# Scores of the later batches in eight 64 by 32 tiles of TensorE, one query copy there, and a new order of the first chunk, in a fused attention and softplus FFN

## The chip, the cores and the metric

The kernel runs on one core of a Trainium2 chip. The metric is the device time of one execution in microseconds, the median of three runs; a profiled execution beside them gives the trace.

## What is computed

Attention over 8 batches, 8 heads, 576 positions and 64 dimensions, with two kinds of mask, followed by a feed-forward layer with a softplus between two matrix products, all in float32. The stride is 32; x is 4608 x 512, w_in 512 x 2048, w_out 2048 x 512:

```python
scores = scale * np.matmul(q, k.transpose(0, 1, 3, 2))
...
mask_local = (rel >= 0) & (rel < stride)
mask_strided = (rel >= 0) & (pos[None, :] % stride == pos[:, None] % stride)
masks = np.stack([mask_local if h < H // 2 else mask_strided for h in range(H)], axis=0)
scores = np.where(masks[None, :, :, :], scores, -1000000000.0)
scores = scores - np.max(scores, axis=-1, keepdims=True)
attn = np.exp(scores)
attn = attn / (np.sum(attn, axis=-1, keepdims=True) + 1e-09)
...
x = np.ascontiguousarray(attn_out.transpose(0, 2, 1, 3)).reshape(B * S, H * D)
...
h = x @ w_in
g = np.maximum(h, 0.0) + np.log1p(np.exp(-np.abs(h)))
return (g @ w_out).astype(np.float32)
```

## The kernel before

**Attention.** Two heads make a pair, so there are 4 pairs to a batch and 32 in all, numbered n = 0 to 31. The host sorts positions so that both masks become bands: a block of 32 queries sees 64 neighbouring keys. A pair's scores are 9 chunks in two places (partitions 0 to 63 and 64 to 127 of an accumulator), 18 matmuls in all. `SPLIT` parts the chunks into part 0 (chunks 0 to 5) and part 1 (chunks 6 to 8). The four pairs of the first batch write both parts into the banks `py` and get their mask from TensorE (L336). From pair 4 on, part 0 goes into bank `ps` and part 1 into the upper half of bank `po`, and VectorE adds the mask (L412). Then come maxima, exponentials, sums, the division, and 16 transposes on VectorE into `pt` (L466). The weighted sums (L534) of a pair share TensorE's turn with the scores of the next pair: that is a joint step.

**Query copies.** A score matmul (L351) contracts over 128 partitions, 64 of head 0 and 64 of head 1. So that the heads stay apart, the queries are laid out in blocks: `lay_out_q` (L261) copies each head's 64 rows into its own columns of `qT` (two copies of 64x576 to a pair), and the other columns hold zeros, written once by the task `z4`. The stationary operand is then 128x64 (two heads by 32 queries), the output 64 partitions high.

**Feed-forward.** 4608 tokens in 9 chunks of 512. For each chunk 16 steps f: `hidden` (L638, 12 matmuls of 128x128 by 512 in fp32r, splitting x and the weights into a high and a low part), `log_part` on ScalarE (L650, L653, L655), softplus on VectorE (L659), `g_high` and `g_low`, and `output` (L678, 12 matmuls into the four banks `py`).

**What sets the order.** Each engine works through its instructions in the order in which the program issues them. For the first chunk, the first two batches and all weight loads, the order is the list `FIRST`. Its names are tasks: q, k, v load a pair's operands (SyncE's queue), D30 is pair 3's query copy for head 0, S31 pair 3's scores of part 1, X, Y, E, Z, x, r, R, M its softmax, T and C the early transposes, V, H, L the weighted sums and the high and low part of x, J4 the scores of pair 4; wi9 loads a piece of `w_in`, ai9, Bi9, di9, hi9, li9 unpack and split it; F, A, u, G, O are the feed-forward steps. `ON_POOL` and `ON_VECTOR` name the tasks that run on GpSimd or VectorE in place of their usual engine. For the rest, `Plan` places tasks by urgency and cost: every four feed-forward steps one task `S{n}` with the scores of pair n and the weighted sums of pair n - 1. `Q{n}` is the query copy, on ScalarE.

Of the kernel before, what the change touches and what calls it, by code (L numbers as in the profile page):

```python
# [35 lines left out]
q0 k0 v2 mask q1 k1 D00 q2 D11 q3 D01 z4 W S01 D21 wi9 X01 k2 D10 Y01 D30 S00 E01 S10 S11 X00 Z01  # L36
Y00 D20 E00 X10 S21 k3 Y10 Z00 ai9 D31 X11 Bi9 wi0 E10 r0 R0 x11 M0 di9 X21 E11 Z10 S20 S30 Y21 E21
ai0 r1 T02 X20 T01 R1 wi3 C02 S31 v0 Y20 X30 hi9 v1 wi1 T00 M1 C01 E20 li9 Y30 ai3 X31 Z20 T11 C00
Z21 V01 x31 r2 T12 V00 C11 H01 wi2 E30 R2 Bi3 M2 E31 T10 L01 C12 V11 C10 Z30 H00 T22 di3 L00 T21
Bi0 wi4 r3 V10 H11 R3 L11 M3 C22 C21 di0 ai1 H10 T20 C20 V21 T32 L10 hi0 v3 H21 T31 Bi1 wo2 C32 ai2  # L40
wo0 V20 L21 T30 H20 C31 q4 C30 li0 L20 V31 hi3 k4 di1 wi6 V30 H30 ai4 H31 li3 hi1 Fa0 ao0 L30 D40
Bi2 L31 F0 Bo0 Bi4 di2 wi5 di4 li1 A0 ao2 Fa1 D41 wi8 wo1 hi4 J4 Ae0 Al0 Bo2 F1 u0 hi2 Gh0 wo4 li4
ai6 li2 A1 wi11 do0 Ae1 ho0 q5 Gl0 Y40 F4 Bi6 lo0 Al1 Y41 A4 do2 u1 wo6 di6 ai5 X4 wo11 Ae4 Gh1 ho2
ao1 Gl1 s4 Al4 O0 v4 u4 Fa2 E4 Bo1 Fa3 hi6 Gh4 do1 li6 wo3 lo2 r4 F2 ho1 F3 ao4 k5 ai11 Gl4 lo1
wo13 Bi5 O1 di5 R4 Bi11 A2 Ae2 Al2 u2 ai8 wi12 A3 di11 Ae3 Bo4 wo8 Gh2 Al3 M4 hi11 do4 wo5 wi10 Gl2
hi5 ho4 li5 F6 A6 D50 u3 li11 Ae6 ao3 P4 ao8 Al6 wo9 lo4 u6 wo15 Bo3 wi7 Bi8 Gh6 wi13 D51 O2 wi14
Gh3 F5 Gl3 A5 ao6 J5 do3 di8 hi8 O4 Bo6 H41 li8 L41 Ae5 wo10 Bo8 ho3 Al5 Y50 H40 k7 Y51 ai10 u5 F9
do6 X5 Bi10 s5 lo3 q6 k6 ai7 Gh5 E5 F8 Gl5 L40 ho6 di10 r5 lo6 hi10 A8 ao5 Gl6 Bi7 do8 O3 li10 Ae8
di7 Bo5 Al8 ai14 hi7 ho8 A9 lo8 wo12 Ae9 O6 u8 F10 do5 R5 Bi14 Al9 li7 M5 Gh8 u9 ai12 ao10 wo7 v5
ho5 Gl8 Bi12 D61 F7 Gh9 A10 Ae10 wi15 O8 Gl9 Al10 P5 D60 u10 lo5 ao9 wo14 Bo10 di12 A7 di14 Gh10  # L50
Gl10 Ae7 Bo9 hi14 J6 Y61 do10 Al7 hi12 u7 H51 O5 li12 ho10 Y60 X6 Gh7 ai13 L51 s6 li14 F11 E6 do9
lo10 ao7 Bi13 A11 di13 r6 Gl7 v6 Bo7 R6 H50 Ae11 M6 Al11 ai15 ho9 F12 k8 q7 do7 lo9 L50 A12 Ae12
hi13 D71 u11 P6 Al12 O10 F14 u12 Gh11 D70 li13 O9 ao14 Bi15 Gl11 J7 di15 A14 Gh12 hi15 ho7 ao15 lo7
Ae14 Y71 Al14 ao11 Y70 li15 u14 ao12 H61 Gl12 X7 O7 s7 Gh14 Bo11 do11 Bo12 L61 Bo14 E7 ho11 do14
Bo15 F13 q8 H60 A13 Gl14 r7 Ae13 lo11 R7 F15 Al13 ho14 L60 do12 u13 ho12 O11 A15 M7 v7 lo12 Qa0
lo14 O12 P7 Ae15 do15 V70 Gh13 k9 Al15 u15 D80 H70 L70 V71 Gh15 H71 v8 D81 L71 O14 Q1 ao13 Bo13
Gl13 QA1 do13 ho13 Qu1 lo13 ho15 Qh1 Gl15 Ql1 O13 Q0 lo15 q9 QA0 O15 Qu0 Qh0 y1 Ob15 Ql0 y0 y2 y3
# [3 lines left out]
D21 D30 r0 r1 hi9 x31 r3 hi0 hi1 ho0 ho2 hi6 D51 Gh3 ho6 r5 Gh8 ho5 D61 ho10 s6 ho9 hi13 ho7 s7  # L61
Gh14 ho11 Gh13 Gh15 ho13 ho15
""".split()
ON_VECTOR = """
D00 D01 z4 D10 C12 M3 C31 li3 D41 hi4 li2 Gl0 lo0 Gl1 Gh4 li6 lo2 Gl4 lo1 hi11 Gl3 li8 Gl5 lo6 hi10
Gl6 li10 ho8 lo8 Gl10 hi14 lo10 Gl7 hi15 lo7 Gl12 Gl14 lo11 D81 y0
# [50 lines left out]
def attention_softplus_ffn(  # L117
# [71 lines left out]
    qT = const.tile([P, 2 * S], F32, name="qT")  # L189
# [32 lines left out]

    def is_local(n):
        return order[n][1] < NPAIR // 2

    def q_of(n):
        return qT_early[n] if n < NPAIR else qT

    def k_of(n):
        return kT_early[n] if n < NPAIR else kT[n % 2]  # L230

    def pt_of(n, a):

        if n in (1, 3):
# [84 lines left out]
    def scores(n, part):  # L319
# [25 lines left out]
        if masked and n > 0:  # L345
            add(True)
# [677 lines left out]
```

## Time and profile before

| | |
|---|---|
| median of 3 runs | 888.06 us (887.53 to 888.86) |
| the profiled execution | 887.86 us, of which span 886.1 us |
| TensorE's granted clock, mean | 0.998 |
| L678 output, busy | 358.5 + 224.1 us |
| L638 hidden, busy | 355.1 + 224.1 us |
| scores from pair 4 on (L351 into ps and po), busy | 25.7 + 14.6 us |
| query copies into qT on ScalarE, busy | 65.6 us in 52 copies |

Times are microseconds of one execution, counted from its first instruction. PE is TensorE, PEld its weight loads, DVE VectorE, ACT ScalarE, POOL GpSimd, SP the engine that issues nearly all DMAs. Busy times of groups overlap and do not add up to the span. A matmul's length in a row is from its start to its modelled end and is longer than the time for which it holds TensorE; what a stretch costs is read from the starts, or from the chain of waits, which follows the work that ended last back to its releasers.

### The profile page before, as it was taken

What the parts mean: (1) busy time and instruction counts of PE and PEld (TensorE: products, weight loads), DVE (VectorE), ACT (ScalarE), POOL (GpSimd) and SP (SyncE); (2) the same over time, 40 slices, a digit from 0 to 9 for tenths busy, and PEclk for the clock granted to TensorE, in tenths of its full rate; (3) what the DMA queues carried; (4) which work ended last, traced back from release to release, by engine and by line L of the source; (5) the groups of instructions that cost most, each with busy time, mean ns of one, the idle gap of its engine ahead of it and who ended that gap; (6) DMA issues with size and microseconds to landing.
All of it is one profiled execution on the core that took longest, in us unless ns stands there. A gap on an engine that the chain in (4) does not pass through costs nothing.

```text
span 886.1 us, 14289 instructions
## 1 busy us (share of the span) xinstructions
PE 874.9 (99%) x5618; PEld 722.5 (82%) x5618; DVE 583.5 (66%) x1289; ACT 432.9 (49%) x762; POOL 71.1 (8%) x92
## 2 busy tenths in 40 slices
PE   7999999999999999999999999999999999999998
PEld 6788888888888888888888888888888888888886
DVE  7899967888766677777766676667777333333332
ACT  6887954544545444544544545444543333333332
POOL 6346550000000000000000000000000000000000
PEclk9999999999999999999999999999999999999999
DMA  9892202211211121111211121112100010001001
GB/s 331 290 371 102 70 31 75 75 46 44 92 45 44 31 76 44 44 45 45 78 45 44 44 92 45 29 31 78 58 18 18 1 48 1 0 1 48 1 0 48
DMA packets 50082, 58.26 MB, mean 66 GB/s; under 512 B 3168, under 2 KB 35296, under 8 KB 50016
## 3 DMA queue, kind: packets, MB, share of 16 engines
q1 hardware_dynamic: 49728, 57.03, 19.8%
q8 instruction: 44, 0.72, 0.3%
q10 hardware_dynamic: 288, 0.33, 0.1%
q14 instruction: 22, 0.18, 0.1%
HBM read 47.91 MB, written 9.44 MB: 65 GB/s over the span
## 4 chain that ended last, share of the span: by engine, by line
PE 97%; DMA 1%; issue 0%; ACT 0%; DVE 0%; SPq 0%; ACTq 0%; DVEq 0%
PE py L678 45%; PE ph L638 44%; PE ps L351 3%; PE pv L534 2%; PE po L534 1%; PE po L351 1%; DMA ri<-in_moe_w_in_dram 1%; PE pt L504 1%; DMA raw_q<-in_qk_dram 0%; PE py L351 0%; ACT a_i L598 0%; DVE a_i L609 0%; PE py L336 0%; DVE qT L261 0%; PE pt L486 0%
## 5 line engine op out<-in xcount | busy, mean ns | idle before, releaser
L678 PE MATMUL py<-w_o,gh 128*128 128x512 f32 x1152 | 358.5, 392 | 0.0
L638 PE MATMUL ph<-x_h,w_i 128*128 128x512 f32 x1152 | 355.1, 389 | 0.0
L650 ACT ACTIVATE u<-ph 128x512 f32<-128x512 f32 x144 | 86.0, 597 | 400.3 <-PE ph L638 397.0
L638 PEld LDWEIGHTS ph<-x_h,w_i 128*128 128x128 f32 x1152 | 215.9, 188 | 45.4 <-issue 0.4
L678 PEld LDWEIGHTS py<-w_o,gh 128*128 128x128 f32 x1152 | 214.0, 188 | 46.6 <-DVE w_o L624 0.2
L638 PE MATMUL ph<-x_l,w_i 128*128 128x512 f32 x576 | 224.1, 389 | 0.0
L678 PE MATMUL py<-w_o,gl 128*128 128x512 f32 x576 | 224.1, 389 | 0.0
L659 DVE SCALAR_TENSOR_TENSOR u<-ph,u 128x512 f32<-128x512 f32 x144 | 99.2, 689 | 176.6 <-ACT u L655 175.0
L466 DVE STREAM_TRANSPOSE pt<-prob 32x192 f32<-32x192 f32 x448 | 137.2, 314 | 6.4
L678 PEld LDWEIGHTS py<-w_o,gl 128*128 128x128 f32 x576 | 108.1, 188 | 22.8
L638 PEld LDWEIGHTS ph<-x_l,w_i 128*128 128x128 f32 x576 | 108.1, 188 | 22.6
L671 DVE TENSOR_TENSOR gl<-u,gh 128x512 fp32r<-128x512 f32 x138 | 95.4, 692 | 11.8 <-DVE gh L261 0.9
L653 ACT ACTIVATE u<-u 128x512 f32<-128x512 f32 x144 | 91.2, 633 | 4.3
L655 ACT ACTIVATE u<-u 128x512 f32<-128x512 f32 x144 | 91.1, 632 | 4.4
L261 ACT COPY qT<-prob 64x576 f32<-64x576 f32 x52 | 65.6, 1261 | 1.0 <-DMA prob<-in_qk_dram 0.7
L261 DVE CAST gh<-u 128x512 fp32r<-128x512 f32 x129 | 54.9, 425 | 10.3
L412 DVE TENSOR_TENSOR prob<-ps,mask_b 128x384 f32<-128x384 f32 x28 | 15.6, 556 | 49.3 <-PE ps L351 49.3
L351 PEld LDWEIGHTS ps<-kT,qT 128*64 128x64 f32 x672 | 21.9, 137 | 10.2 <-issue 8.8
L351 PE MATMUL ps<-kT,qT 128*64 128x64 f32 x672 | 25.7, 226 | 0.3 <-DVE qT L261 0.3
L412 DVE TENSOR_TENSOR prob<-po,mask_b 128x192 f32<-128x192 f32 x28 | 10.0, 356 | 19.6 <-ACT x_h L572 19.6
L570 DVE TENSOR_TENSOR x_l<-pv,x_h 128x288 fp32r<-128x288 f32 (+2 forms) x44 | 17.4, 407 | 5.7 <-ACT x_h L572 5.5
L427 ACT ACTIVATE prob<-prob 128x576 f32<-128x576 f32 x24 | 16.5, 688 | 9.1 <-DVE prob L421 9.1
(102 smaller groups left out, 507.0 us busy)
## 6 DMA issues: line engine op xcount, KB each, us to landing
v_in<-in_v_dram SPq DMA_DIRECT2D x28, 320.0 KB, 3.6
out_dram<-o SPq DMA_DIRECT2D x35, 256.0 KB, 2.1
ri<-in_moe_w_in_dram SPq DMA_DIRECT2D x16, 512.0 KB, 7.8
ro<-in_moe_w_out_dram SPq DMA_DIRECT2D x16, 512.0 KB, 8.2
prob<-in_qk_dram SPq DMA_DIRECT2D x28, 288.0 KB, 2.7
kT<-in_qk_dram SPq DMA_DIRECT2D x28, 288.0 KB, 3.0
v_in<-in_v_dram SPq DMA_DIRECT2D x28, 48.0 KB, 2.7
room<-in_v_dram SPq DMA_DIRECT2D x4, 320.0 KB, 5.9
```

Of the source, the lines that this page charges most:

```text
L261: (engine.copy if engine is nc.scalar else engine.tensor_copy)(dst, src)
L351: nc.tensor.matmul(ps[rows[place], 64 * (x - lo) : 64 * (x - lo) + 64], lhsT=blocks_of(n)[:, c // 32].rearrange("p h l -> p (h l)"), rhs=k ...
L412: nc.vector.tensor_tensor(pv, sv, m, op=ALU.add)
L466: nc.vector.transpose(pt[32 * (i + c) : 32 * (i + c) + 32, h, a : a + hi - lo, 32 * i : 32 * i + 32,], src[:, lo:hi, 32 * c : 32 * c + 32],)
L534: nc.tensor.matmul(po[64 * h : 64 * h + 64, TILE * x : TILE * x + TILE], lhsT=vs[n][:, a, h, :], rhs=pt_of(n, a)[:, h, a % 2], start=True, ...
L638: nc.tensor.matmul(ph, lhsT=w32["i", f][:, half, cc * P : (cc + 1) * P], rhs=x_of(x, cc)[:, t0 : t0 + n], start=(i == 0), stop=(i == 3 * N ...
L650: nc.scalar.activation(us[c, f], phs[c, f], AF.Abs)
L653: nc.scalar.activation(u, u, AF.Exp, scale=-1.0)
L655: nc.scalar.activation(u, u, AF.Ln, bias=1.0)
L659: nc.vector.scalar_tensor_tensor(u, in0=phs.pop((c, f)), scalar=0.0, in1=u, op0=ALU.max, op1=ALU.add)
L671: engine.tensor_tensor(g, us.pop((c, f)), ghs[c, f].bitcast(F32), op=ALU.subtract)
L678: nc.tensor.matmul(py[t], lhsT=g[:, sl], rhs=w32["o", f][:, half], start=(f == 0 and n == 0), stop=(f == NFC - 1 and n == 2),)
```

## The change

Three parts.

1. From pair 4 on, `head_scores` takes the place of `scores`. It issues one matmul for each head: 64 rows (that head's dimensions), 32 columns (32 queries), 64 keys streamed; 36 matmuls to a pair. The output of chunk, place and head goes to the 32 partitions from 64 * place + 32 * `place_of(part, h)`. In part 0 head 0 comes first, in part 1 head 1, so that the four tiles of part 0 and the four of part 1 are eight different tiles of the 128x128 array. Chunks 0 to 2 are issued alone (four tiles), then 3 with 6, 4 with 7, 5 with 8. `prob_transposes` reads the rows accordingly. The first batch keeps its 128x64 scores.
2. As the heads no longer stand side by side in one operand, `qT` holds the queries once: `lay_out_q` is one copy of 128x576, the zeros (`z4`) go, and the tasks D40 and D41 become D4 (the same for 5 to 8).
3. `FIRST`, `ON_POOL` and `ON_VECTOR` are new.

```diff
 FIRST = """
-q0 k0 v2 mask q1 k1 D00 q2 D11 q3 D01 z4 W S01 D21 wi9 X01 k2 D10 Y01 D30 S00 E01 S10 S11 X00 Z01
...
+mask q0 k0 q1 W D00 k1 D10 q2 q3 D01 S01 X01 D11 D20 Y01 S00 S11 X00 S10 Y00 E01 Z01 k2 D31 D21 S20
...
-    qT = const.tile([P, 2 * S], F32, name="qT")
+    qT = const.tile([P, S], F32, name="qT")
...
     def lay_out_q(n, heads=(0, 1), engine=nc.scalar):
 
+        if n >= NPAIR:
+            to = qT.rearrange("p (m l) -> p m l", l=32)
+            copy_on(engine, to, raws[n].rearrange("p (l m) -> p m l", l=32))
+            return
...
+    def place_of(part, h):
+
+        return 1 - h if part == 1 else h
+
+    def head_scores(n):
+
+        taken.append(n)
+        pss[n, 0] = ps_s.tile([P, 512], F32, tag="ps", name=f"ps_{n}")
+        shared[n] = ps_o.tile([P, 512], F32, tag="po", name=f"po_{n}")
+        pss[n, 1] = shared[n][:, S // 2 :]
+        for x in range(6):
+            for chunk in (x, x + 3) if x > 2 else (x,):
+                part = chunk // 6
+                for place in range(2):
+                    a, i = block_at(chunk, place)
+                    c = TILE * a + 32 * i
+                    for h in range(2):
+                        to = 64 * place + 32 * place_of(part, h)
+                        head = slice(64 * h, 64 * h + 64)
+                        at = 64 * (chunk - SPLIT[part][0])
+                        nc.tensor.matmul(
+                            pss[n, part][to : to + 32, at : at + 64],
+                            lhsT=qT[head, c : c + 32],
+                            rhs=k_of(n)[head, c : c + 64],
+                            start=True,
+                            stop=True,
+                        )
...
-                for lo, hi in ((0, 6), (6, 9)):
+                for part, (lo, hi) in enumerate(SPLIT):
+                    row = 64 * place + 32 * place_of(part, h)
+                    src = p[row : row + 32]
...
     def joint_scores(n):
 
-        scores(n, 0)
-        scores(n, 1)
+        head_scores(n)
...
-    task("z4", zeros, NPAIR, of("z4", nc.gpsimd))
...
         def work(i=i, n=n):
-            scores(n, 0)
-            scores(n, 1)
+            head_scores(n)
```

On TensorE, the first joint step of the program (pair 5's scores, then pair 4's weighted sums); the rows give line, operation, output, operands, output size and how many follow each other. Before:

```order
L638 MATMUL ph_5_932<-x_h_592,w_i_856 128x512 x2
L638 MATMUL ph_5_932<-x_l_612,w_i_856 128x512
L351 MATMUL ps_0_951<-kT_101,qT 64x64 x12
L351 MATMUL po_964<-kT_101,qT 64x64 x6
L534 MATMUL po_964<-pt,v_in 64x96 x6
L534 MATMUL pv_977<-pt,v_in 64x96 x6
L678 MATMUL py_104<-w_o_858,gh_4_785 128x512 x2
```

After:

```order
L699 MATMUL py_107<-w_o_774,gl_2_925 128x512
L373 MATMUL ps_978<-kT_101,qT 32x64 x16
L373 MATMUL po_979<-kT_101,qT 32x64 x4
L373 MATMUL ps_978<-kT_101,qT 32x64 x4
L373 MATMUL po_979<-kT_101,qT 32x64 x4
L373 MATMUL ps_978<-kT_101,qT 32x64 x4
L373 MATMUL po_979<-kT_101,qT 32x64 x4
L555 MATMUL po_979<-pt,v_in 64x96 x6
L555 MATMUL pv_1022<-pt,v_in 64x96 x6
L659 MATMUL ph_9_1046<-x_h_363,w_i_888 128x512 x2
```

The 12 + 6 matmuls of 64 partitions have become 24 + 12 of 32 partitions, the last three rounds alternating between the two banks; the weighted sums stand behind them as before.

On SP, which issues the loads, the first rows of the program (raw_q0 to raw_q3 are the queries of pairs 0 to 3; early_l0, l2, l1, l3 the keys of pairs 0, 1, 2, 3; room_2 the values of pair 2; ri_9 a piece of w_in). Before:

```order
L258 DMA raw_q0_149<-in_qk_dram 128x576
L279 DMA early_l0_91<-in_qk_dram 128x576
L290 DMA room_2_111<-in_v_dram 96x128
L297 DMA room_2_111<-in_v_dram 128x5x128
L258 DMA raw_q1_155<-in_qk_dram 128x576
L279 DMA early_l2_93<-in_qk_dram 128x576
L258 DMA raw_q2_159<-in_qk_dram 128x576
L258 DMA raw_q3_162<-in_qk_dram 128x576
L578 DMA ri_9_186<-in_moe_w_in_dram 128x4x128
```

After:

```order
L255 DMA raw_q0_150<-in_qk_dram 128x576
L280 DMA early_l0_91<-in_qk_dram 128x576
L255 DMA raw_q1_153<-in_qk_dram 128x576
L280 DMA early_l2_93<-in_qk_dram 128x576
L255 DMA raw_q2_168<-in_qk_dram 128x576
L255 DMA raw_q3_170<-in_qk_dram 128x576
L280 DMA early_l1_95<-in_qk_dram 128x576
L280 DMA early_l3_97<-in_qk_dram 128x576
L599 DMA ri_1_276<-in_moe_w_in_dram 128x4x128
```

The values of pair 2 and the piece 9 of w_in, which stood among the queries and keys, now stand behind all of them.

On ACT, the rows from the first query copy on (early_h2, h1, h3 are the laid-out queries of pairs 1, 2, 3). Before:

```order
L261 COPY early_h2_92<-raw_q1_155 64x32x18
L377 ACTIVATE early_l0_91<-early_l0_91 128x3x64
L261 COPY early_h1_94<-raw_q2_159 64x18x32
L377 ACTIVATE early_l0_91<-early_l0_91 128x6x64
L598 ACTIVATE a_i_9_249<-ri_9_186 128x512
L261 COPY early_h3_96<-raw_q3_162 64x32x18
```

After:

```order
L258 COPY early_h2_92<-raw_q1_153 64x18x32
L397 ACTIVATE early_l0_91<-early_l0_91 128x3x64
L258 COPY early_h1_94<-raw_q2_168 64x32x18
L397 ACTIVATE early_l0_91<-early_l0_91 128x6x64
L258 COPY early_h3_96<-raw_q3_170 64x18x32
L397 ACTIVATE early_l2_93<-early_l2_93 128x6x64
```

The scaling of weight piece 9 between the copies for pairs 2 and 3 is gone, so pair 3's copy follows pair 0's second exponential directly; the other halves of pairs 2 and 3 are on GpSimd before and after.

81 lines of the change are left out of this document (36 added, 45 removed).

## The prediction

> **What bounds the kernel now.** I read the page first, down to its chain of waits.
>
> ```profile
> span 886.1 us, 14289 instructions
> PE 874.9 (99%) x5618; PEld 722.5 (82%) x5618; DVE 583.5 (66%) x1289; ACT 432.9 (49%) x762; POOL 71.1 (8%) x92
> ...
> PE 97%; DMA 1%; issue 0%; ACT 0%; DVE 0%; SPq 0%; ACTq 0%; DVEq 0%
> ```
>
> TensorE sets the end: 97% of the chain is its own work. Work on DVE, ACT or POOL is worth time only where TensorE waits for it. So next come its three long waits, in square brackets at the end of rows of the timeline, and the busy time by stretch (stretch, length, then busy us of PE, PEld, DVE, ACT, POOL; granted clock, DMA share, GB/s).
>
> ```profile
> 9.36 0.92 PE L351 MATMUL py<-early_l,early_h 128*64 128x64 f32 x24 [1.86 <-ACT early_h L261]
> 12.46 0.91 PE L351 MATMUL py<-early_l,early_h 128*64 128x64 f32 x12 [1.67 <-ACT a_i L598]
> 24.00 0.27 PE L504 MATMUL pt<-room,early_l 128*64 128x64 f32 x1 [1.62 <-issue]
> ...
> 36.00:133.00 97.00, 97.00 (x593) 79.49 (x593) 86.66 (x193) 75.40 (x182) 50.42 (x48) 1.00 0.46 165
> 133.00:690.00 557.00, 557.00 (x3624) 461.03 (x3623) 400.77 (x921) 264.90 (x416) 0.00 (x0) 1.00 0.17 51
> ```
>
> From 36 to 690 us TensorE has no gap at all (97.00 of 97.00, 557.00 of 557.00). The long waits, 1.86, 1.67 and 1.62 us, lie in the first 36 us. So the change can gain in two ways: a shorter score block on TensorE, 28 times over, and a denser head.
>
> **The score block.** The chain of waits around one joint step (last hidden layer, scores, weighted sums, output layer):
>
> ```profile
> 255.11 2.72 PE ph L638 x12
> 257.83 0.85 PE ps L351 x24
> 258.68 0.35 PE po L351 x12
> 259.02 0.50 PE po L534 x12
> 259.52 0.49 PE pv L534 x12
> 260.02 2.94 PE py L678 x12
> ...
> L351 PE MATMUL ps<-kT,qT x672: 222/222/270, 34.5 to 669.4; 128*64 128x64 f32 x168
> L351 PE MATMUL po<-kT,qT x336: 222/222/222, 35.3 to 669.7; 128*64 128x64 f32 x168
> ```
>
> The kernel issues 18 score matmuls to a pair, the trace counts 36 (672 + 336 over 28 pairs): a float32 matmul is two passes. The steady po part runs 12 passes in 0.35 us. Two tiles of 64 columns are in use, so 6 passes follow each other on each and **a pass holds its tile 58 ns**. All 36 are 18 x 0.058 = 1.05 us; the block takes 0.85 + 0.35 = 1.20, so 0.15 is the change from the 128x128 shape to the 128x64 shape. Going back costs 2.94 - 2.72 = 0.22.
>
> That tiles run beside each other, each at its own pace, stands in the head's timeline (start, length, then the operation):
>
> ```profile
> 15.86 0.24 PE L486 MATMUL pt<-room 128*64 128x128 bf16 x2
> 15.91 0.65 PE L504 MATMUL pt<-room,early_l 128*64 128x64 f32 x16
> ...
> 18.56 0.25 PE L534 MATMUL pv<-pt,room 128*64 128x96 f32 x1
> 18.62 0.22 PE L504 MATMUL pt<-room,early_l 128*64 128x64 f32 x1
> 18.65 0.36 PE L534 MATMUL pv<-pt,room 128*64 128x96 f32 x4
> ```
>
> Two 128-column matmuls take 0.05 us together, as long as one pass of 58 ns. And at 18.56 a weighted sum (L534) begins on one tile while the other still has a transpose (L504) to start at 18.62.
>
> After the change there are 36 matmuls to a pair, 72 passes, each over half the rows and half the columns. A pass still streams 64 columns, so I keep 58 ns. The six chunks of part 0 use four tiles: 6 matmuls, 12 passes on each, 12 x 0.058 = 0.70 us. Part 1's three chunks use the other four tiles and fit beside the last three rounds (6 passes, 0.35). New is a second change of shape, from 64x32 to the weighted sums' 128x64. No row shows that pair of shapes; the nearest are 0.15 and 0.22, and I take 0.15, since it leads into the same shape as the 0.15 row. **New block: 0.15 + 0.70 + 0.15 = 1.00, a gain of 0.20** in the 26 joint steps (pairs 5 to 7, 9 to 31). Pairs 4 and 8 have no weighted sums behind the scores and gain 1.05 - 0.70 = 0.35. Sum: 26 x 0.20 + 2 x 0.35 = **5.9 us**.
>
> The bounds: with the second change of shape free, 26 x 0.35 + 0.7 = 9.8; at 0.22, 26 x 0.13 + 0.7 = 4.1. What no row shows is tiles that differ in their rows, or more than two at once; if only two ever run, the passes take 36 x 0.058 = 2.10 and the block is slower (a rival below).
>
> **The query copies.**
>
> ```profile
> L261 ACT COPY qT<-prob x52: 1242/1258/1280, 31.9 to 648.4; 64x576 f32<-64x576 f32 x52
> L219 DVE MEMSET qT<- x2: 538/538/538, 5.8 to 6.5; 64x576 f32 x2
> ...
> L412 DVE TENSOR_TENSOR prob<-ps,mask_b 128x384 f32<-128x384 f32 x28 | 15.6, 556 | 49.3 <-PE ps L351 49.3
> ```
>
> One copy over 128 partitions replaces two over 64, from the second batch on: about 28 x 1.26 = 35 us less copying, nearly all on ACT. It is worth nothing in the loop, because TensorE never waits there. The DVE transposes and mask adds keep their number and sizes. Both parts of the scores now end together, so the first mask add cannot begin ahead of the second part; DVE has room for that (400.77 busy of 557.00). If that cover were gone, one mask add, 0.56 us by its row, would stand in each step. The two memsets go, which belongs to the head.
>
> **The head.** Here the order counts. The rows of ACT and POOL at the two early waits, the loads by size, and the stretches:
>
> ```profile
> 8.14 1.16 ACT L261 COPY early_h<-raw_q 64x576 f32<-64x576 f32 x1 [5.76 <-DMA raw_q<-in_qk_dram]
> ...
> 9.60 1.25 ACT L261 COPY early_h<-raw_q 64x576 f32<-64x576 f32 x1
> ...
> 11.67 0.66 ACT L598 ACTIVATE a_i<-ri 128x512 f32<-128x512 f32 x1 [0.39 <-DMA ri<-in_moe_w_in_dram]
> 12.35 1.23 ACT L261 COPY early_h<-raw_q 64x576 f32<-64x576 f32 x1
> ...
> 9.64 2.52 POOL L261 COPY early_h<-raw_q 64x576 f32<-64x576 f32 x2 [3.11 <-DMA raw_q<-in_qk_dram]
> ...
> ri<-in_moe_w_in_dram SPq DMA_DIRECT2D x16, 512.0 KB, 7.8
> ...
> room<-in_v_dram SPq DMA_DIRECT2D x4, 320.0 KB, 5.9
> ...
> room<-in_v_dram SPq DMA_DIRECT2D x4, 48.0 KB, 6.1
> ...
> 8.00:12.00 4.00, 1.43 (x40) 1.24 (x40) 3.66 (x9) 3.44 (x5) 2.30 (x2) 0.98 1.05 387
> 12.00:14.00 2.00, 1.54 (x25) 1.52 (x27) 1.76 (x7) 1.95 (x3) 1.37 (x3) 0.50 1.08 383
> 14.00:16.00 2.00, 2.00 (x51) 1.95 (x49) 1.81 (x5) 1.95 (x9) 1.38 (x4) 0.68 1.14 355
> 16.00:20.00 4.00, 3.97 (x127) 3.89 (x124) 3.23 (x10) 3.36 (x8) 3.11 (x5) 1.00 1.10 371
> 20.00:24.00 4.00, 2.38 (x75) 2.24 (x70) 4.00 (x10) 2.47 (x11) 1.18 (x2) 1.00 1.09 393
> ```
>
> The DMA engines are full here (share 1.05 and more). The first wait (to 9.36 us) is for pair 1's query, copied at 8.14; ahead of it stand the 48 + 320 KB of a value load, 377 kB at 387 GB/s = 1.0 us. The new order sends values and weights behind all queries and keys: 1.0 earlier. The second wait (from 10.79, 1.67 before 12.46) is for pair 3's second half, copied on ACT at 12.35, behind a weight scaling that itself stood behind its 512 KB load. In the new order ACT has no weight work there, and pair 3's halves follow pair 2's on ACT and POOL. The first copies then run from 9.60 - 1.0 = 8.6 to 9.85, the second to 11.1. TensorE, itself 1.0 earlier, ends pair 1 at 9.8, works some 1.2 us on pair 2 (36 passes on two tiles, 1.05, and mask adds), and meets pair 3 at 11.1: about 1.6 of the 1.67 is gone. Together 2.6. DVE is nearly full after that (10.80 busy of 12 us from 12 to 24), and though it sheds two memsets (1.08), I take 0.3 off: **2.3 us**. The third wait (1.62, where nothing in the profile released TensorE) I leave as it is. The weight loads that now come later on SP cost nothing as long as the first weights are ready by the first hidden layer; one load of w_in stands before the values and one among them, so I count none.
>
> Clock: after the two gaps it reads 0.50 and 0.68, about 2 x 0.50 + 2 x 0.32 = 1.6 us of TensorE time lost. I count no gain there, because DVE would bind instead. The Trainium skill, page "TensorE: Matmul & The Clock Gate", section "What's actually happening", says that the clock drops to half after an idle window of some 3.4 us and knows nothing between half and full. The 0.50 agrees; by that rule the denser head never throttles, and the sum would come out up to 1.6 lower.
>
> Ends for the head: 2.3 + 1.6 (clock) + 1.6 (third wait gone) = 5.5 of gain; a second stall like the third wait leaves 0.7; and an order that gains nothing, 0.
>
> **Sum.** The profiled execution took 887.86 us (span 886.1, 1.8 around it), 0.2 below the median of the runs. 887.86 - 5.9 - 2.3 = **879.7 us**. Its own range is 876 (9.8 and 2.3, or 5.9 and 5.5, about) to 883 (4.1 and 0.7).
>
> **Rivals.**
> - *The head gains nothing* (DVE binds, or a new wait): 887.86 - 5.9 = 882.0. For it: DVE's 4.00 of 4.00 from 20 to 24 us. Against it: both waits named above have their cause moved.
> - *Eight tiles never run at once*, only four: then part 1's passes come on top, 0.15 + 1.05 + 0.15 = 1.35 in place of 1.20, 26 x 0.15 = 3.9 lost, nothing won in the two others. With the head 887.86 + 3.9 - 2.3 = 889.5. No row shows more than two tiles at work, which leaves it open.
> - *Tiles of the two row halves take turns on one accumulator bank*: in part 0 the heads sit in different row halves and write into one bank. If they alternate, 12 passes become 24, 1.40 us, and the block 1.70: 26 x 0.50 + 2 x 0.35 = 13.7 lost, 887.86 + 13.7 - 2.3 = 899.3, **slower**. It decides from 0.90 us of passes on (0.15 + 0.90 + 0.15 = 1.20). For it speaks no row; every tile today spans all rows. Against: today's two tiles write different partitions of one bank and do not hinder each other. The Trainium skill, page "TensorEngine Tiling (Array Packing)", section "Restrictions and Gotchas", says that different row tiles cannot use the same PSUM bank at the same time; no run here shows it yet.
> - *Passes start no faster than now*, one every 29 ns: 72 take 2.10, the change does not do what it says, 26 x 1.20 + 2 x 1.05 = 33.3 lost, 918.9. The starts at 18.62 and 18.65 on tiles of their own speak against a common beat. The first page named, section "Wait — 56ns, not 53.3ns?", gives a floor of about 25 ns between starts; by it, an estimate, 72 passes take 1.8 us and the kernel ends near 910.
>
> **Chances.** Forecast 0.65, head gains nothing 0.17, four at once 0.07, bank turns 0.06, no faster starts 0.05. The first two are faster by over 0.2% (1.8 us, about what a measurement here can tell from no change): 0.82. Four at once lies within: 0.06, the other 0.01 of it with the slower ones, 0.12. The first two hold 0.82, so the range is theirs: 875.5 to 886.0, its upper end past 882.0 by 4, for a head that loses a stall or two.
>
> **What would show it.** Right: the score rows of a joint step sum to 1.0 us in the chain of waits, po's rows lie inside those of ps, the waits on L351's early copies fall to some tenths, and the first hidden matmul starts some 2.3 us earlier than now. Wrong: a block of 1.35 or 1.70 (turns), a longer first row of the weighted sums (the second change of shape), or a new TensorE gap between 12 and 60 us with DVE or a weight load as its releaser.

## The result and the profile after

The changed kernel takes 884.25 us (median, 882.83 to 884.51) against 888.44 (887.53 to 888.86) for the kernel before on the same chip: a ratio of 0.9949, 95% interval 0.9937 to 0.9961. The forecast was 879.7 with a range of 875.5 to 886.0. So it became faster, by about half of what was forecast. The profiled execution took 884.07 us, 3.79 less than that of before; the forecast was 8.2 less.

The page of the changed kernel: the span, the engines' busy time with their instructions, the engines' shares of the chain of waits, the instruction queues, and the query copies.

```profile
span 882.3 us, 16274 instructions
PE 872.7 (99%) x6626; PEld 717.4 (81%) x6626; DVE 585.7 (66%) x1283; ACT 403.0 (46%) x742; POOL 65.8 (7%) x88
...
q8 instruction: 52, 0.85, 0.4%
...
PE 93%; DMA 2%; DVE 2%; ACT 1%; issue 1%; POOL 0%; SPq 0%; ACTq 0%; POOLq 0%
...
L258 ACT COPY qT<-prob 128x576 f32<-128x576 f32 x26 | 33.2, 1278 | 1.5 <-DMA prob<-in_qk_dram 1.5
```

TensorE still sets the end. It has 1008 score passes more (28 pairs x 36), and as many weight loads. ACT is 29.9 us less busy. The query copies alone fell by 32.4 us: 52 of 1261 ns (65.6 us) became 26 of 1278 (33.2 us).

The chain of waits around one joint step (start, length, engine, tile, line):

```profile
255.30 0.41 PE ps L373 x20
255.72 0.03 PE po L373
...
256.17 0.12 PE po L373 x8
256.29 0.65 PE po L555 x12
256.94 0.49 PE pv L555 x12
257.43 2.94 PE py L699 x12
...
279.42 0.41 PE ps L373 x20
```

The score rows run from 255.30 to 256.29, 0.99 us in place of 1.20. The first row of the weighted sums grew from 0.50 to 0.65; that is the second change of shape, 0.15. The block is 1.14: a gain of 0.06, where 0.20 was forecast. The way back to 128x128 costs the same as before (2.94). From score row to score row (here 255.30 to 279.42) a joint step takes 24.11 us in place of 24.17, as the median over the loop; this is called the joint period below.

The head: stretches (length, busy us of each engine with its instructions, granted clock, DMA share, GB/s), and TensorE's long waits there, in brackets at the end of the timeline's rows.

```profile
0.00:12.00 12.00, 9.87 (x145) 6.02 (x147) 8.80 (x19) 6.58 (x9) 8.97 (x34) 1.00 0.87 306
12.00:16.00 4.00, 2.68 (x84) 2.44 (x80) 3.92 (x14) 2.94 (x11) 2.11 (x3) 1.00 1.13 355
...
36.00:133.00 97.00, 96.61 (x701) 79.12 (x700) 88.04 (x189) 74.46 (x183) 47.09 (x44) 1.00 0.47 166
133.00:690.00 557.00, 557.00 (x4509) 458.45 (x4509) 403.05 (x921) 234.49 (x391) 0.00 (x0) 1.00 0.17 51
...
7.89 0.57 PE L343 MATMUL py<-early_l,early_h 128*64 128x64 f32 x12 [0.25 <-issue]
9.90 0.92 PE L343 MATMUL py<-early_l,early_h 128*64 128x64 f32 x24 [0.26 <-issue]
...
16.48 0.27 PE L525 MATMUL pt<-room,early_l 128*64 128x64 f32 x2 [1.42 <-issue]
...
22.40 0.22 PE L525 MATMUL pt<-room,early_l 128*64 128x64 f32 x1 [1.36 <-issue]
...
27.54 0.73 PE L659 MATMUL ph<-x_h,w_i 128*128 128x512 f32 x2
```

The waits of 1.86 and 1.67 us on the early copies have become tenths, and the clock stays at 1.00, where it read 0.50 and 0.68 from 12 to 16 us. But where one wait of 1.62 us had no releaser (such waits are called stalls below), there are now two, of 1.42 and 1.36. The first hidden matmul starts at 27.54 us, against 29.19 before: 1.65 earlier, where 2.3 was forecast. Behind the head a gap of 0.4 us is new, at 75 us (96.61 busy of 97.00).

Two things were open. Why do the score passes take 0.84 us (0.99 less the 0.15 for the first change of shape) and not 0.70? And what is the head worth by itself, with its two stalls? The experiments go after one, then the other.

### The profile page after: what moved, and what is told of

Same layout as the page of the kernel before. It is cut to its first block, busy times and chain, and to the rows that moved or that the text cites. A ratio compares the mean times of both kernels' runs of the same rounds, so it can differ in the third digit from the quotient of the medians.

```text
span 882.3 us, 16274 instructions
## 1 busy us (share of the span) xinstructions
PE 872.7 (99%) x6626; PEld 717.4 (81%) x6626; DVE 585.7 (66%) x1283; ACT 403.0 (46%) x742; POOL 65.8 (7%) x88
## 4 chain that ended last, share of the span: by engine, by line
PE 93%; DMA 2%; DVE 2%; ACT 1%; issue 1%; POOL 0%; SPq 0%; ACTq 0%; POOLq 0%
PE py L699 43%; PE ph L659 42%; PE pv L555 2%; DMA ro<-in_moe_w_out_dram 2%; PE ps L373 2%; PE po L555 2%; PE po L373 1%; PE pt L525 1%; DVE pt L487 0%; DMA raw_q<-in_qk_dram 0%; ACT prob L453 0%; DVE early_h L258 0%; DVE u L680 0%; DVE a_o L630 0%; ACT early_h L258 0%
## 5 line engine op out<-in xcount | busy, mean ns | idle before, releaser
L487 DVE STREAM_TRANSPOSE pt<-prob 32x192 f32<-32x192 f32 x448 | 140.2, 317 | 6.7
L692 DVE TENSOR_TENSOR gl<-u,gh 128x512 fp32r<-128x512 f32 x135 | 93.3, 691 | 10.6
L258 ACT COPY qT<-prob 128x576 f32<-128x576 f32 x26 | 33.2, 1278 | 1.5 <-DMA prob<-in_qk_dram 1.5
L373 PEld LDWEIGHTS ps<-kT,qT 64*32 64x32 f32 x1344 | 23.3, 106 | 9.9 <-issue 9.2
L373 PE MATMUL ps<-kT,qT 64*32 64x64 f32 x1344 | 27.8, 220 | 0.0
L373 PE MATMUL po<-kT,qT 64*32 64x64 f32 x672 | 22.0, 227 | 0.0
```

Of the source, the lines that this page charges most:

```text
L258: (engine.copy if engine is nc.scalar else engine.tensor_copy)(dst, src)
L373: nc.tensor.matmul(pss[n, part][to : to + 32, at : at + 64], lhsT=qT[head, c : c + 32], rhs=k_of(n)[head, c : c + 64], start=True, stop=True,)
L487: nc.vector.transpose(pt[32 * (i + c) : 32 * (i + c) + 32, h, a : a + hi - lo, 32 * i : 32 * i + 32,], src[:, lo:hi, 32 * c : 32 * c + 32],)
L692: engine.tensor_tensor(g, us.pop((c, f)), ghs[c, f].bitcast(F32), op=ALU.subtract)
```

## Experiments on the score passes

**Rounds of six.** The twelve matmuls of part 1 are spread over all six rounds, two to a round.

```diff
         for x in range(6):
-            for chunk in (x, x + 3) if x > 2 else (x,):
+            for chunk in (x, 6 + x // 2):
                 part = chunk // 6
-                for place in range(2):
+                for place in (range(2), (x % 2,))[part]:
```

> Six rounds of six matmuls in place of three of four and three of eight: in each round the four of part 0, then two of part 1 (both heads of one place, the places taking turns). A tile of part 0 comes again after 12 passes and not after 16. In the changed kernel the 72 passes of a joint score block took about 0.85 us and the block 1.14. Window theory (TensorE looks only about 16 passes ahead; with eight tiles in a round the second pass of a tile blocks all that stand behind it): the passes run at 56 ns on every tile of part 0, 12 x 0.056 + 0.03 = 0.70 us, block 0.99, joint period 24.11 - 0.15 = 23.96, kernel 28 x 0.15 = 4.2 us less than the changed kernel, near 880.0. Rival A, a floor of about 12 ns a pass as soon as more than four tiles are used: 72 x 0.012 = 0.86, no gain, 884.2. Rival B, two tiles over one another in the same columns hinder each other: the same 12 matmuls of part 1 still share columns with part 0, so the loss stays, 0.86, 884.2.

Measured: 881.42 us, ratio 0.9916 (0.9901 to 0.993). One score block in its chain of waits:

```profile
277.25 0.19 PE ps L373 x4
...
278.10 0.06 PE po L373 x2
278.15 0.65 PE po L555 x12
```

The score rows take 0.90 in place of 0.99, and the joint period is 24.03. The gain is 0.09, between the 0.15 of the window theory and the zero of rivals A and B. None of the three holds as it was put.

**Rounds of four only**, and **four with two tiles in the same columns.** In the first, part 1 comes after all of part 0:

```diff
-        for x in range(6):
-            for chunk in (x, x + 3) if x > 2 else (x,):
+        for x in range(9):
+            for chunk in (x,):
```

> The six rounds of part 0 first, then the three of part 1, never more than four tiles at a time: 9 rounds x 2 x 0.056 = 1.01 us of passes, plus 0.03, so 0.18 more than the changed kernel's 0.85: block 1.32, joint period 24.29, kernel 28 x 0.18 = 5.0 us more, near 889.3. All theories say this; if it takes less, passes on a tile are quicker than 56 ns, if the same as the changed kernel, the rounds of eight gave nothing at all.

In the second, each of the first six rounds has two matmuls of part 0 and two of part 1, one above the other in the same columns:

```diff
-        for x in range(6):
-            for chunk in (x, x + 3) if x > 2 else (x,):
+        for x in range(9):
+            round_ = [(x - 3, place, h) for place in range(2) for h in range(2)]
+            if x < 6:
+                column = x // 3
+                round_ = [(x % 3 + 6 * o, p, column ^ o) for p in range(2) for o in range(2)]
+            for chunk, place, h in round_:
...
```

> Nine rounds of four as in the run beside it, but in the first six of them two tiles stand over one another in the same columns (one matmul of part 0 and one of part 1, from the two halves of the rows, into two banks); the computation is the same. Window theory and rival A (floor per pass): only four tiles at a time, so the same 1.01 + 0.03 us of passes as the run beside it, kernel within 0.5 us of that one, near 889.3. Rival B (tiles in the same columns hinder each other): in the changed kernel three rounds of eight with four such pairs each lost 0.17 us over the 0.67 hoped for, 0.014 a pair and more if pairs take turns; here 12 pairs at turns cost up to 12 x 0.056 = 0.67 more, at least 0.17, kernel 4.8 to 19 us above the run beside it.

Measured: 884.41 us (ratio 0.9952, 0.9937 to 0.9967) and 884.51 (0.9951, 0.9934 to 0.9967), joint period 24.16 in both. Rival B falls: tiles in the same columns cost nothing. But both runs are 5 us below what all theories said, and about level with the changed kernel; as their joint period is that of the kernel before (24.17), what they gain lies outside the joint steps. The chain of the first shows how:

```profile
255.65 0.64 PE ps L373 x36
256.29 0.03 PE po L373
...
256.46 0.23 PE po L373 x13
256.69 0.65 PE po L555 x12
```

The passes took 1.04 - 0.15 = 0.89 us and not 1.04. The first pass of part 1 is the 49th in the program, yet it starts after only 36 passes of part 0: it overtakes 12. (How far TensorE starts later passes past waiting ones is called its look-ahead here.) So part 1 slides over the last rounds of part 0, though no round has more than four matmuls. The timeline of the changed kernel shows the same number:

```profile
303.46 0.48 PE L373 MATMUL ps<-kT,qT 64*32 64x64 f32 x20
303.73 0.24 PE L373 MATMUL po<-kT,qT 64*32 64x64 f32 x1
```

There the first pass of part 1 is the 33rd, and it starts after 20. In both orders the first pass of part 1 went past 12 waiting passes and no more. The same two rows show the rate of the rounds of four: 20 passes in five groups of four, the first 21 starts within 0.27 us. That is the forecast's 56 to 58 ns per pass on each of four tiles.

**Part 1 first, and part 1 brought forward.** Two more orders: in the first, shown against the rounds of six, part 1's matmuls stand ahead in each round; in the second, against the changed kernel, the rounds have 7, 7, 6, 6, 6 and 4 matmuls:

```diff
-            for chunk in (x, 6 + x // 2):
+            for chunk in (6 + x // 2, x):
```

> Rounds of six as in the earlier run of six, but the two matmuls of part 1 ahead of the four of part 0 in each round. There the tiles of part 0 started a pass every 14.7 ns (56 / 4 = 14.0 at best), and after the last of them came two passes of part 1, 0.057 us. Window theory: the tiles of part 0 set the end, the tail goes and the start is 14 ns later: passes 0.72 in place of 0.756 us, joint period 24.03 - 0.04 = 23.99, kernel 1 us below the run of six. Rival (a rate of 10.5 ns a pass whatever the order, 72 x 10.5 = 756): no change, 24.03.

```diff
-        for x in range(6):
-            for chunk in (x, x + 3) if x > 2 else (x,):
+        late = [(6 + y, p, h) for y in range(3) for p in range(2) for h in range(2)]
+        for x, many in enumerate((3, 3, 2, 2, 2, 0)):
+            round_ = [(x, place, h) for place in range(2) for h in range(2)] + late[:many]
+            late = late[many:]
+            for chunk, place, h in round_:
...
```

> Rounds of 7, 7, 6, 6, 6 and 4 matmuls: the twelve of part 1 brought forward, none in the last round. Window theory: a tile of part 0 comes again after at most 14 passes, still inside 16, so these tiles go on at 14 to 14.7 ns a pass to the end and nothing follows them: passes 0.69 to 0.70 us in place of 0.756, joint period 23.97, kernel 1.5 us below the run of six. Rival (10.5 ns a pass whatever the order): 0.756, 24.03, no change.

Measured: 880.96 us (ratio 0.9912, 0.9896 to 0.9929) and 880.72 (0.9912, 0.9897 to 0.9927), joint period 24.03 in both. The window theory's gains of 0.04 and 0.06 a step did not come: three orders give the same 24.03. So something besides the tiles and the look-ahead seems to hold the passes to a rate; the next run tests that.

**Twice the passes for the same columns.** Each matmul of the rounds of six is cut into two of 32 keys.

```diff
-        for x in range(6):
+        for x, side in ((x, side) for x in range(6) for side in range(2)):
...
-                at = 64 * (chunk - SPLIT[part][0])
+                at = 64 * (chunk - SPLIT[part][0]) + 32 * side
+                k0 = c + 32 * side
                 nc.tensor.matmul(
-                    pss[n, part][to : to + 32, at : at + 64],
+                    pss[n, part][to : to + 32, at : at + 32],
                     lhsT=qT[head, c : c + 32],
-                    rhs=k_of(n)[head, c : c + 64],
+                    rhs=k_of(n)[head, k0 : k0 + 32],
```

> The rounds of six once more, but each matmul cut into two of 32 keys: in each round first the six lower halves, then the six upper ones. The same columns stream through the same tiles, in 144 passes in place of 72. In three orders of six and seven the 72 passes took 0.756 us, 10.5 ns each. Rate theory (TensorE takes up passes, or their weight loads, no faster than one in 10.5 ns once its look-ahead is used up): 144 x 10.5 = 1.51 us, joint period 24.03 + 0.76 = 24.79, kernel 28 x 0.76 = 21 us above the run of six, near 902. Rival (the streaming in the tiles sets it, tiles hindering each other while they stream): the columns are the same, 0.76 to 0.85 us, kernel at most 3 us above the run of six, 881 to 884.

Measured: 901.35 us (ratio 1.0135, 1.0088 to 1.0181), joint period 24.51. Its chain of waits gives the whole block, and its timeline a stretch in the middle:

```profile
258.54 0.16 PE ps L374 x4
...
259.89 0.65 PE po L556 x12
```

```profile
308.12 0.23 PE L374 MATMUL ps<-kT,qT 64*32 64x32 f32 x4
308.15 0.21 PE L374 MATMUL po<-kT,qT 64*32 64x32 f32 x1
308.17 0.19 PE L374 MATMUL ps<-kT,qT 64*32 64x32 f32 x1
308.17 0.21 PE L374 MATMUL po<-kT,qT 64*32 64x32 f32 x1
308.18 0.21 PE L374 MATMUL ps<-kT,qT 64*32 64x32 f32 x2
308.20 0.19 PE L374 MATMUL po<-kT,qT 64*32 64x32 f32 x1
308.20 0.21 PE L374 MATMUL ps<-kT,qT 64*32 64x32 f32 x1
308.22 0.19 PE L374 MATMUL po<-kT,qT 64*32 64x32 f32 x1
308.22 0.23 PE L374 MATMUL ps<-kT,qT 64*32 64x32 f32 x4
```

The score rows take 1.35 us, 0.45 more than with half the passes and the same columns. So the number of passes counts, and the rival (streaming) falls. The tiles are not what is full here either: at the start of this block (307.54, 307.57, 307.60 us) part 0's four tiles took a pass each every 0.03 us, and in the stretch shown each takes two in 0.10. The rate is not the 10.5 ns of the expectation, though. The rows repeat after 0.10 us (308.12 to 308.22) with 4 + 1 + 1 + 1 + 2 + 1 + 1 + 1 = 12 passes in between, and that is six matmuls of two passes: **one matmul every 16.7 ns**. All 72 at that rate are 1.20 us, which is 1.35 less the 0.15 for the change of shape. The profiled execution took 898.75 us, 18.3 more than that of the rounds of six (880.46): 28 x 0.48 = 13.4 from the blocks, 1.5 by the first hidden matmul, and 3.1 in stalls without a releaser between 482 and 560 us, of the kind looked at below.

For the blocks of 64 columns 16.7 ns a matmul is not the whole account. Thirty-six matmuls at that rate are 0.60 us, and one part 0 tile's twelve passes 0.67; the runs of six measured 0.75, 0.08 above the larger of the two. The changed kernel would spend 3 x 0.112 = 0.34 us on its rounds of four, where the tiles are the limit, and then 24 x 0.0167 = 0.40 on its rounds of eight, by this estimate 0.74; it measured 0.84. What the remaining 0.08 and 0.10 are, no run shows. What the runs do show is the difference of the orders: part 1's tiles have work from the first round in the runs of six, and that is worth 0.09. What makes the 16.7 ns (taking up instructions, or loading weights) these runs don't tell apart.

## Experiments on the head

**The new scores with the old order.** The changed kernel with the order and engines of the first chunk from before. In the first version the one query copy of a pair stood where the second half had stood (pair 8's on VectorE, as that half had been), in the second version where the first half had stood, all on ScalarE. The second version's list against that of the kernel before (pairs 4 and 5 shown):

```diff
-wo0 V20 L21 T30 H20 C31 q4 C30 li0 L20 V31 hi3 k4 di1 wi6 V30 H30 ai4 H31 li3 hi1 Fa0 ao0 L30 D40
-Bi2 L31 F0 Bo0 Bi4 di2 wi5 di4 li1 A0 ao2 Fa1 D41 wi8 wo1 hi4 J4 Ae0 Al0 Bo2 F1 u0 hi2 Gh0 wo4 li4
+wo0 V20 L21 T30 H20 C31 q4 C30 li0 L20 V31 hi3 k4 di1 wi6 V30 H30 ai4 H31 li3 hi1 Fa0 ao0 L30 D4
+Bi2 L31 F0 Bo0 Bi4 di2 wi5 di4 li1 A0 ao2 Fa1  wi8 wo1 hi4 J4 Ae0 Al0 Bo2 F1 u0 hi2 Gh0 wo4 li4
...
-hi5 ho4 li5 F6 A6 D50 u3 li11 Ae6 ao3 P4 ao8 Al6 wo9 lo4 u6 wo15 Bo3 wi7 Bi8 Gh6 wi13 D51 O2 wi14
+hi5 ho4 li5 F6 A6 D5 u3 li11 Ae6 ao3 P4 ao8 Al6 wo9 lo4 u6 wo15 Bo3 wi7 Bi8 Gh6 wi13  O2 wi14
```

> The new scores with the first chunk's order and engines of the kernel before (the query copies of the later pairs as one, where their second half stood). The two parts of the change add: the scores alone are worth what the joint periods show, 24.17 - 24.11 = 0.06 x 26, and what pairs 4 to 8 gave, about 2 us, kernel near 886.4; first hidden matmul at 29.2 as before, early waits of 1.86, 1.67 and 1.62 us back. Rival: the new order only fits the new scores or the other way round; then the kernel is at 888.4 or above.

> The new scores with the first chunk's order of the kernel before, the single query copies now where the first of the two halves stood, on ScalarE. The earlier run of this kind stood 1.94 us at 60.88 for the query copy of pair 5, which came late. If that wait was the reason why it gained nothing: the wait is gone, the scores are worth 28 x 0.06 = 1.7 us, kernel near 887 (ratio 0.998). Rival (the new scores make the old first chunk slower in another way, its early waits above all, 2.24 us against 1.86): again 888.6 or above, with first hidden matmul at 30 or later.

Measured: 889.54 us (ratio 1.0008, 0.9999 to 1.0018) and 885.21 (0.9952, 0.9938 to 0.9967). The two versions, which differ in the place of five copies, are over 4 us apart. The waits of the first version name 2.3 us of it, and the row behind them has the longest one:

```profile
PE ps L372 <- ACT qT L257: 2.3, 2, 1.9
...
62.81 0.37 PE L372 MATMUL ps<-kT,qT 64*32 64x64 f32 x12 [1.94 <-ACT qT L257]
```

With the copies in time these waits are gone and the old order holds nearly the whole gain. By the spans it is 883.1 us, against 886.1 before and 882.3 for the changed kernel: 3.0 us with the new scores and their single copy, 0.8 more with the order. Not all of the 3.0 is the scores': the first hidden matmul starts at 28.58 us here, 0.6 earlier than before, and at 30.56 in the first version, whose clock was lower in the head (see the rows of both below).

**The old scores with the new order.** The kernel before, with the changed lists; D4 to D8 are again two halves each (shown against the list of the changed kernel).

```diff
-C30 do1 V31 hi1 q4 li1 V30 Fa0 wo2 ai4 Bi4 H30 L30 ho1 ai2 di4 H31 ao0 L31 D4 Bo0 F0 wi3 hi4 Fa1
+C30 z4 do1 V31 hi1 q4 li1 V30 Fa0 wo2 ai4 Bi4 H30 L30 ho1 ai2 di4 H31 ao0 L31 D40 D41 Bo0 F0 wi3 hi4 Fa1
```

> The new order and engines of the first chunk with the scores of the kernel before (each later pair again with two query copies in place of one, at the same place in the order). If the parts add: the score blocks of the changed kernel save 0.06 us each by the joint periods (24.17 to 24.11), 28 x 0.06 = 1.7 us of the 4.2; the first chunk has the other 2.5: kernel near 886.0, first hidden matmul near 27.5. Rival (each order fits only its own scores): the doubled copies on ScalarE hold up scores or outputs of the first chunk, and no more than half of it is left, 887.3 or above.

Measured: 887.21 us, ratio 0.9987 (0.9977 to 0.9996). The first hidden matmul starts at 26.89, but the first chunk has new waits:

```profile
PE ph L638 <- DVE u L659: 1.5, 3, 0.6
PE ps L351 <- ACT qT L261: 0.4, 1, 0.4
```

By the first hidden matmul 2.3 us were won against the kernel before; of these 1.5 are lost again to DVE (the changed kernel loses 0.4 there) and 0.4 to the query copy. So the order is worth 1.2 us with the old scores (0.0013 of 888.65). The rival was nearer: the order fits its own scores better.

**The order's worth once more.** The scores of 7, 7, 6, 6, 6, 4 with the old order, beside the changed kernel itself.

> The rounds of 7, 7, 6, 6, 6 and 4 with the first chunk's order of the kernel before (query copies as in the second run of that kind). What is the new order of the first chunk worth once the scores are the new ones? If the 2.3 us forecast for it hold: 2 us or more above the 880.7 of the same scores with the new order, ratio to the kernel before 0.9912 + 0.0025 = 0.9937. If it is worth what the earlier pair of profiles shows (spans of 883.1 with the old order, 882.3 with the new one): 0.3 to 0.9 us above, ratio 0.9916 to 0.9922. Score blocks as in the run of 7, 7, 6, 6, 6, 4: joint period 24.03.

> The changed kernel itself once more, beside the run above, for the size of the order's worth: ratio to the kernel before 0.9949 as first measured, against 0.9952 for the same scores with the old order. If the new order is worth 2.3 us, its ratio comes out near 0.9926; if 0.3 to 0.9, within 0.994 to 0.995. First hidden matmul between 26.1 and 27.6 us, stalls at the 449th and 705th instruction of 0.5 to 1.6 us each, as in the seven profiles with this order so far.

Measured: 884.41 us (ratio 0.9951, 0.9937 to 0.9965; joint period 24.05) and 883.32 (0.9939, 0.9924 to 0.9954). With the scores of 7, 7, 6, 6, 6, 4 the new order is worth 3.5 us, across two sets of runs (0.9951 - 0.9912 = 0.0039 of 889). With the scores of the change it is 1.2 by the changed kernel's repeat (0.9952 - 0.9939) and 0.3 by its first runs (0.9952 - 0.9949); the intervals are as wide as these differences. Neither answer expected fits both. Part of the spread lies in the old order itself. These rows show the old order with the scores of 7, 7, 6, 6, 6, 4, then in the second version and in the first: a long wait, and the granted clock (third from the end of each second row) from 12 to 16 us.

```profile
11.94 0.91 PE L343 MATMUL py<-early_l,early_h 128*64 128x64 f32 x12 [1.92 <-DMA early_l<-in_qk_dram]
...
12.00:16.00 4.00, 4.00 (x88) 3.89 (x90) 3.50 (x11) 3.19 (x10) 3.05 (x4) 0.66 1.12 369
```

```profile
11.78 0.57 PE L343 MATMUL py<-early_l,early_h 128*64 128x64 f32 x12 [1.70 <-DMA early_l<-in_qk_dram]
...
12.00:16.00 4.00, 3.83 (x124) 3.72 (x122) 3.57 (x12) 3.98 (x13) 2.97 (x4) 1.00 1.12 370
```

```profile
10.26 1.35 PE L342 MATMUL py<-early_l,early_h 128*64 128x64 f32 x24 [2.24 <-ACT early_h L257]
...
12.00:16.00 4.00, 3.01 (x50) 2.69 (x50) 3.73 (x11) 3.40 (x10) 3.08 (x3) 0.50 1.10 369
```

In three of four profiles with the old order (before among them) the clock falls to half, each time for 3.4 us or twice that. It is not the length of one wait alone. In the kernel before the clock stayed at 1.00 through the wait of 1.86 us and fell at 11.9 us, within the next one, of 1.67. With the scores of 7, 7, 6, 6, 6, 4 it fell at 11.4, within the wait of 1.92 that followed two of 0.9, and again at 25.0, behind a stall of 1.89. In the first version it fell at 10.5, right behind the wait of 2.24, and stayed at 1.00 through the wait of 1.94 that ended at 62.81. In the second version waits of 1.20, 0.98 and 1.70 left it at 1.00. With the new order it read 1.00 from 12 to 16 us in every profile. That fits the new order winning more where the old one loses its clock, and little where it does not.

**The two stalls.** Dummies are matmuls whose result nobody reads; the program issues ten ahead of the first scores. Here there are sixty-four more, each narrower, so that the stretch is as long but 128 instructions are ahead of everything.

```diff
-            nc.tensor.matmul(idle, lhsT=warm[:, :P], rhs=warm, start=True, stop=True)
+            nc.tensor.matmul(idle[:, :72], lhsT=warm[:, :P], rhs=warm[:, :72], start=True, stop=True)
...
-    first["W"] = lambda: dummies(10)
+    first["W"] = lambda: dummies(74)
```

> The changed kernel with 74 dummies of 72 columns in place of 10 of 512 ahead of the first scores: about as long, 4.4 us, but 128 TensorE instructions more (a weight load and a matmul each). In the changed kernel TensorE stood at its 449th and its 705th instruction, 256 apart, 1.42 and 1.36 us, both times with its program still on the way (a 16384 byte packet of the instruction queue landed 1.4 us before it went on). Fetch theory: the stalls stay at the 449th and the 705th instruction and so come 128 instructions earlier in the program: one at the first transposes (12.4 us, where 0.38 is waited anyway), one near 18.6 us, perhaps a third near 24.5; no stall at 15.06 and 21.04; kernel within -0.5 to +1.5 us of 884.2. Rival (the transposes wait for data there): both stalls stay at the same transposes with the same lengths, 884.2.

Measured: 884.07 us, ratio 0.995 (0.9935 to 0.9965). In the changed kernel the stretches up to the two stalls hold these numbers of instructions (in parentheses behind PE and PEld):

```profile
0.00:15.10 15.10, 12.55 (x221) 8.45 (x222) 11.83 (x29) 9.25 (x19) 11.03 (x35) 1.00 0.93 317
15.10:21.10 6.00, 4.56 (x128) 4.38 (x128) 3.97 (x12) 4.45 (x15) 2.11 (x4) 1.00 1.09 341
```

That is 443 up to the first and 256 up to the second. (The 449 and 705 of the expectation count TensorE's six semaphore records too.) With the dummies:

```profile
0.00:17.03 17.03, 14.62 (x349) 13.40 (x350) 13.75 (x35) 11.38 (x28) 12.33 (x37) 1.00 0.95 313
17.03:22.05 5.02, 4.62 (x128) 4.32 (x127) 4.65 (x10) 4.02 (x12) 2.21 (x5) 1.00 1.00 337
...
PE pv L555 <- issue: 1.9, 2, 1.7
PE pt L507 <- issue: 0.2, 1, 0.2
```

Again a stall stands after 349 + 350 = 699 instructions, but at other work: bf16 transposes (0.16 us), 128 instructions earlier in the program. The next is 255 later, in the weighted sums, at 22.01 us (1.69 us). The one at 443 falls together with the wait at 12.37 that was there anyway. No transposes of L525 stand without a releaser any more. So the stalls belong to the count of instructions, 256 from one to the next, and the instruction queue brings them in packets of 0.85 MB / 52 = 16 KB (the page's q8 row above). That the queue is TensorE's shows in the number of packets: 52 for its 13252 matmuls and weight loads, 44 for the 11236 of the kernel before, one for every 256. The rival falls.

A packet's landing ends each stall: in all 14 profiles, at the 29 stalls of 0.41 to 1.89 us, TensorE went on 1.2 to 1.6 us after the queue's last packet had landed, however long it had stood. What sets the landing, and why it takes that long to go on, no run shows.

In the run with the dummies the stalls from 16 us on add up to 2.1 us (0.16, 0.21 and 1.69), and the time is the same. The one stall of the kernel before (1.62) stood at the same count, after 349 + 349. The three later profiles with the old order have stalls at both counts (0.41 to 1.89 us). In the nine profiles of the new order with ten dummies the stalls at 443 and 699 are between 0.54 and 1.63 us long. The changed kernel's first profile has 1.42 and 1.36, its repeat 0.71 and 0.81, a difference of 1.26 out of the 1.35 us between the two profiled executions (884.07 and 882.72).

## Why the prediction was right, and where it was off

Faster was forecast at 0.82, and the time lies in the range, 4.6 us above the forecast itself. Both gains that were added up came out smaller in these runs, 0.06 for 0.20 a joint step and 1.65 for 2.3 in the head. The upper end of the range was drawn for a head that gains nothing or loses a stall or two, and it held a miss of another kind, in the score blocks: that part is luck.

- **Score block: the mechanism right, one term too small.** "12 x 0.058 = 0.70 us" for the passes measured 0.84. It took part 1's passes to fit beside part 0's at no cost, and a round of eight to run like a round of four. A tile does turn in 56 to 58 ns. But part 1 starts late, as its passes get past no more than 12 that wait; orders that give it work from the first round win 0.09 of the 0.14. And matmuls are taken up at a limited rate: one per 16.7 ns, as the run with 72 matmuls shows, makes eight 0.134 us, not 0.112, or 0.07 over the three rounds of eight. How the two share the 0.14, and what holds the three better orders at 0.75, stays open. Over 28 blocks the 0.14 is 3.9 us: nearly all of the 4.4 by which the profiled execution (884.07) missed 879.7. The rest of the step held: 0.15 into the scores, 0.15 for the second change of shape, 0.22 back.
- **Query copies: right.** The copies cost ACT 32 us less, and in the loop TensorE has no wait on ACT to lose (557.00 of 557.00). Their place in the first chunk does matter, as the first run with the old order showed.
- **Head: 2.3 forecast, 1.65 at the first hidden matmul.** The two named waits went as argued. The third wait, "I leave as it is", was the weak step: it goes with the count of instructions, TensorE runs into it twice in all nine profiles of the new order with ten dummies, and its length changes from one execution to the next. In the changed kernel's repeat the two add up to 1.52 us in place of 2.78, and the first hidden matmul starts at 26.25 us, 2.9 earlier than before. So the 2.3 lies between two profiles of the same kernel, and that it is near them is partly luck. The gap at 75 us (0.4, released by DVE's u) is the new wait that "What would show it" named, if later. The order alone is worth 0.3 to 1.2 us with the new scores and 1.2 with the old ones; with the scores of 7, 7, 6, 6, 6, 4 it was 3.5. The 2.3 lies within that spread too, which these runs don't narrow.
- **Clock: "I count no gain there"** left something out. In the new order the clock did not fall: it read 1.00 from 12 to 16 us in all ten profiles. By the Trainium skill, page "TensorE: Matmul & The Clock Gate", section "What's actually happening", the clock drops after an idle window of some 3.4 us, so that a denser head does not throttle, and the trace agrees. But it fell here with shorter waits than that (1.86 and 1.67 us, with 1.43 us of work between them, in the kernel before), and the measured ones decide. How much of the 1.65 us this is, no run separates. The executions of the kernel before give an idea: those whose mean granted clock was 0.999 or 1.000 (8 of the 44 with a clock on record) took 887.8 us in the mean, those at 0.994 to 0.996 (33) took 889.1. Up to 1.3 us goes with the clock, the longer waits that lower it included.
- **Rivals.** Bank turns: fell. The heads of part 0, in the two row halves, write to one bank, and 20 of their passes start in 0.27 us; at turns a block would be 1.70 and not 1.14. So the rule of the Trainium skill, page "TensorEngine Tiling (Array Packing)", section "Restrictions and Gotchas", does not hold here for tiles that write different partitions of one bank. Passes no faster than one in 29 ns: fell, 72 in 0.84 us are one in 12. The Trainium skill's floor of about 25 ns between starts (page "TensorE: Matmul & The Clock Gate", section "Wait — 56ns, not 53.3ns?") does not hold between tiles; the measured 12 ns decide. Only four at once: nearest to the truth of the rivals, since the runs of four only are about as fast as the change, but at 1.19 us a block and not 1.35, because the last rounds overlap by themselves.

**A faster version.** The rounds of six, and of 7, 7, 6, 6, 6, 4, beat both kernels: 0.9916 (0.9901 to 0.993) and 0.9912 (0.9897 to 0.9927) of the time before, 880.7 to 881.4 us. Rounds of six need two changed lines.

## What to carry to other kernels

In these runs small tiles on TensorE gave parallel passes only as far as it looked ahead and took up matmuls: spread the matmuls that use the otherwise idle tiles evenly from the first round, and count matmuls times the rate at which they are taken up (16.7 ns here) beside passes times tile time. A search of an order makes gains that belong to that order; test an edit under both orders, and look at where its small copies stand. When waits are taken away from the start of a program, ask next whether its instructions arrive in time.

## What the runs showed of the hardware

- Float32 passes of 64x32 tiles start some 7 ns apart on different tiles (in the rounds of six, part 0's four tiles from 301.21 us and part 1's first at 301.24), and hold a tile for some 56 ns at 64 columns (five groups of four in 0.27 us). With six tiles in use and 32 columns the rate settled at one matmul (two passes) per 16.7 ns; in a block of 64 columns it was not measured by itself.
- The first pass for idle tiles overtook 12 passes that waited for theirs (20 of 32 and 36 of 48 had started).
- Tiles above one another in the same columns, writing to two banks, cost nothing (24.16 us a step with and without).
- The granted clock fell to half for 3.4 us, or twice that, within a wait of 1.67 us that followed one of 1.86 after 1.43 us of work, and behind waits of 1.89 and 2.24; it stayed at 1.00 through one of 1.94, and through 1.20, 0.98 and 1.70 within 7 us. So no length of a single wait told here whether it falls.
- TensorE stalled for up to 1.89 us after its 443rd and 699th instruction, 256 apart, where the instructions are short and stand close. The changed kernel's loop shows no such stall (557.00 busy of 557.00); with 72 short matmuls a pair there were some in the loop too (0.5 to 1.3 us). The row of the DMA view for 14 to 16 us in the changed kernel has the packet, which landed 1.4 us before TensorE went on at 16.48:

```profile
q8 instruction: 1, 0.02, 2.9%
```
